# Half a mixer one query block sooner and by seven products, and a shared pair of PSUM banks

## The chip, the cores and the metric

The kernel runs on one core of a Trainium2 chip. The metric is the device time of one execution in microseconds (us), as the median of several executions. TensorE (PE) does the matrix products and their weight loads (PEld), VectorE (DVE) and ScalarE (ACT) empty the PSUM banks, GpSimd (POOL) mostly starts loads, and SyncE (SP) starts transposes by DMA and the stores of the output.

## The reference

Eight batches of 3008 rows go first through a gated attention unit without softmax and then through an MLP-mixer, which works over the rows (tokens) first and over the channels second:

```python
# u, v: (8, 3008, 256), z: (8, 3008, 64), float32
scores = (1.0 / S) * np.matmul(z, z.transpose(0, 2, 1))   # S = 3008
attn = np.maximum(scores, 0.0) ** 2
x = u * np.matmul(attn, v)
# w_tok1 (3008, 256), w_tok2 (256, 3008), w_ch1 (256, 1536), w_ch2 (1536, 256)
h = np.maximum(x.transpose(0, 2, 1) @ w_tok1, 0.0) @ w_tok2
u = x + h.transpose(0, 2, 1)
h2 = np.maximum(u @ w_ch1, 0.0) @ w_ch2
out = (u + h2).astype(np.float32)
```

All products are made in bf16 with sums in float32. Since the scores are symmetric, a block of them that is made for one pair of row blocks serves, transposed, for the other pair too.

## The kernel before

**Blocks.** A batch `b` has six query blocks `q` of 512 rows (the last has 448) and six key groups of four tiles of 128 rows. Below, (b, q) is a query block. `score_run` makes two tiles of a block of scores in one pair of PSUM banks (line 435), `relu` on ACT and `square` on DVE turn them into an `at` tile (lines 473 and 481), and `av_matmul` (line 671) multiplies it with v. From the second batch on, a block of scores above the diagonal is also turned by `flip` (line 540, a DMA transpose on SP) into an `fl` tile for its mirrored pair; the blocks on the diagonal of later query blocks are made as triangles (lines 461, 513, 525). When all six groups of a query block are summed, ACT and DVE add the two halves (lines 798, 804) and gate with u (line 828), and SP turns the result (line 843) into `x_sb`.

**The mixer** of a batch needs all six of its query blocks. Its pieces wait in two lists. `heads` holds `tok1` (line 889, six pieces) and `tok2` (line 908, six pieces; DVE adds their result to xT in line 917, and SP turns that into `u_sb` in line 939). `tails` holds the channel part, six pieces `ch1` for each query block (line 958; their relu goes to ACT in line 1005 or to DVE in line 1007, by which of the two the planner holds to be less loaded), and the second product with w_ch2 in one of two forms:

- the classical form `ch2` (line 1192), four pieces of 12 products of 256 columns for a query block, each two pieces in a PSUM pair `op` of their own, followed by a residual add (line 1206 or 1224) and a store;
- the form `fast` by seven products instead of eight (Winograd's form of Strassen's scheme): 84 products of 128 columns (line 1077) in one PSUM pair `f`, with twelve sums on DVE over h2pre (lines 1030 to 1033) and six adds from `f` (lines 1133 to 1152).

Before the change, `fast` holds for all but the first three query blocks of batch 0 and the very last block. In a batch's last query block (q = 5) only the first 256 rows go by seven products. The rest is classical: one tile of 128 rows in the even batches, and in the odd ones also a tile of the two batches' last 64 rows together. These one or two pieces stand ahead of the products 5, 6, 3 and 7 in the list and take a pair `op`.

**When.** A batch's mixer is made in two halves. The loop at the end of the kernel plans at build time, in the order of PE, with its own estimates of times. `goals` says at which query block which half may start; while a half runs, no attention is picked:

```python
    goals = {(1, 2): (0, 1 + HALF)}
    for b in range(2, B):
        goals[b, 0] = (b - 1, 1 + HALF)
```

So the first half of batch 0 (all of `heads`, and `tails` of its blocks 0 to 2) runs ahead of block (1, 2); from batch 2 on, the second half of the mixer before the last and the first half of the last one run ahead of block (b, 0).

**Room.** There are four PSUM pairs, dealt out by `take_slot`. The twelve `fl` buffers hold both flips and h2pre (three for a query block); `flips_fit` says how many flips may lie in them:

```python
        n = live["fl"] - live["mix"]
        return n < (MIRRORS if b < 2 else AHEAD if in_mixer[0] else ROOM["fl"])
```

with `MIRRORS` 8, `AHEAD` 6 and `ROOM["fl"]` 12. SP's queue is in order; what it starts is planned by `push("sp", ...)`. Loads of u, v and z go by POOL, asked for one at a time, at least 4 us apart (`ask`, `SPACING`).

The functions that the change touches, with the line numbers of the profile:

Of the kernel before, what the change touches and what calls it, by code (L numbers as in the profile page):

```python
# [13 lines left out]
P = 128  # L14
# [43 lines left out]
def kernel(  # L58
# [258 lines left out]
    RES = 6  # L317
    live = {"at": 0, "fl": 0, "xT": 0, "x": 0, "us": 0, "mix": 0, "res": 0}
    ROOM = {"at": 6, "fl": 12, "xT": 9, "x": 6, "us": 3, "res": RES}
    MIRRORS = 8  # L320
    U_TURN = 1
    SUMS_TO_COME = 0.85
    AHEAD = 6
# [207 lines left out]
    def flips_fit(b):  # L531

        n = live["fl"] - live["mix"]
        return n < (MIRRORS if b < 2 else AHEAD if in_mixer[0] else ROOM["fl"])

    def flip(b, q, g, at, uses, done):
        fl = sb.tile([P, GK, QW], BF16, tag="fl", name="fl", bufs=ROOM["fl"])
# [280 lines left out]
    def gate(blk, dh, acc, t):  # L818
        b, q, W = blk.b, blk.q, blk.W
        uT = uTs[b, q]  # L820
        if dh == 0:
            xTs[b, q] = sb.tile([P, DT, QW], BF16, tag="xT", name="xT", bufs=ROOM["xT"])
            live["xT"] += 1
            if W < QW:
                nc.gpsimd.memset(xTs[b, q][:, :, W:], 0.0)
        xT = xTs[b, q]
        full, rest = W // P, W % P
        nc.vector.tensor_mul(  # L828
            xT[:, dh, :full * P].rearrange("p (t s) -> p t s", s=P),
            acc[:, :full * P].rearrange("p (t s) -> p t s", s=P),  # L830
            uT[:, :full, dh, :])
        if rest:
            nc.vector.tensor_mul(
                xT[:, dh, full * P:W], acc[:, full * P:W], uT[:, full, dh, :rest])
        if dh == DT - 1:
            gated[0] += 1
            push("sp", t, 1.25, 7.5 if q < NQ - 1 else 12.0, lambda t: turn_x(b, q, t), first=1,
                 room=lambda: has_room(("x",)) and (b == 0 or mode[0] == "full"))

    def turn_x(b, q, t):  # L840
# [30 lines left out]
    def add_mixer(b):  # L871
# [143 lines left out]

        def fast(q):

            return (b > 0 or q >= NQ // 2) and (b, q) != (B - 1, NQ - 1)

        def columns(q):  # L1020
            return P if q == NQ - 1 else 2 * P
# [31 lines left out]
        PLACE = {1: (0, 0), 6: (0, 0), 7: (0, 0), 4: (0, 1), 2: (1, 0), 5: (1, 1), 3: (1, 1)}  # L1053
        LEFT = {1: (0, 0), 2: (1, 0), 4: (1, 1), 7: (0, 0), 5: (0, 1), 6: (1, 1), 3: (1, 0)}

        def apart(inst, q, writes, bank):

            other = "reads" if writes else "writes"
            own = "writes" if writes else "reads"
            key = f"f{b}_{q}_"  # L1060
            tc.declare_no_dep(inst.ins, group=f"{key}{other}{1 - bank}", reason="other bank")
            tc.add_to_no_dep_group(f"{key}{own}{bank}", inst.ins)

        def matmuls(q, m, c2):

            n = columns(q)
            r, h = PLACE[m]
            to = regions(q)[:, r, h]
            h2, k = st["h2", q, c2 // 2], c2 % 2
            i, half = LEFT[m]  # L1070
            lhs = h2[:, 2 * k + i, half * n:half * n + n]
            if m in (1, 2, 3):
                rhs = w_ch2_sb[:, 2 * c2 + (m > 1), P * (m == 3):P * (m == 3) + P]
            else:
                rhs = w_sums[:, {5: 0, 6: 1, 7: 2, 4: 3}[m], c2, :]
            for j in range(n // P):
                apart(nc.tensor.matmul(  # L1077
                    to[:, j, :], lhs[:, j * P:(j + 1) * P], rhs,
                    start=m in (1, 2) and c2 == 0 and j == 0, stop=c2 == CHT // 2 - 1,
                    skip_group_check=True), q, True, r)  # L1080
# [20 lines left out]
        def piece_over(q):  # L1101
            left[q] -= 1
            if not left[q]:
                n = CHT // 4
                live["fl"] -= n
                live["mix"] -= n
                fl_free.extend([pe[0] + 0.2] * n)

        def done_with_u(q):
            u_left[q] -= 1  # L1110
# [2 lines left out]
        def adds(q, m, end):  # L1113

            us, J, n = st["u", q], columns(q) // P, full_tiles[q]
            f = regions(q)
            a, fifth_at, fourth_at = f[:, 0, 0, :J], f[:, 1, 1, :J], f[:, 0, 1, :J]

            def res(r):
                if st["res", q][r] is None:  # L1120
                    live["res"] += 1
                    st["res", q][r] = sb.tile([P, 2, D], F32, tag="res", name="res", bufs=RES)
                return st["res", q][r].rearrange("p t (h d) -> p t h d", d=P)[:, :J]

            def put(r):
                recent[0] = st["res", q][r][:, 0, :1]
                nc.sync.dma_start(
                    out=rows_of(out[b], q)[:, r * J:(r + 1) * J, :],
                    in_=st["res", q][r][:, :J, :])
                live["res"] -= 1  # L1130

            def first():
                return nc.vector.tensor_add(res(0)[:, :, 0], a, us[:, 0, :J])

            def fifth():
                return nc.vector.tensor_add(res(1)[:, :, 1], fifth_at, us[:, 1, J:2 * J])

            def fourth():
                return nc.vector.tensor_add(res(1)[:, :, 0], fourth_at, us[:, 0, J:2 * J])

            def sixth():
                return nc.vector.tensor_add(res(0)[:, :, 1], a, us[:, 1, :J])

            def third():
                o = res(0).rearrange("p t h d -> p h t d")
                inst = nc.vector.tensor_add(o, f[:, 1, :, :J], o)  # L1146
                put(0)
                return inst

            def seventh():  # L1150
                o = res(1).rearrange("p t h d -> p h t d")
                inst = nc.vector.tensor_add(o, a.unsqueeze(1).to_broadcast([P, 2, J, P]), o)
                put(1)
                return inst

            busy = 0.16 + 0.00105 * J * P * (1 + (m in (3, 7)))
            fn = {1: first, 5: fifth, 4: fourth, 6: sixth, 3: third, 7: seventh}[m]
            after_ = {7: (5, 4), 3: (1, 6)}.get(m, ())

            def room():  # L1160
                if m in (1, 5, 4) and st["res", q][m != 1] is None and not has_room(("res",)):
                    return False
                return all(read[q, k].t is not None for k in after_)

            def run(t):
                apart(fn(), q, False, PLACE[m][0])
                st["reads", q].append(t)
                if m in (3, 7):
                    free["sp"] = max(free["sp"], t) + 0.4
                if len(st["reads", q]) == 6:  # L1170
                    st["freed", q].t = max(st["reads", q])
                    done_with_u(q)

            push("dve", max(end + 0.21, known(st["turned", q])), busy, busy + 0.13, run,
                 first=1, done=read[q, m], room=room)

        def ch2(q, half, i, end):
            apart = alone(q, half)
            if i == 0 or apart:
                st["o_slot"], _ = take_slot()  # L1180
# [80 lines left out]
        def ch2_pieces(q, key):  # L1261
            out = []
            for half in halves(q)[1 if fast(q) else 0:]:
                for i in range(pieces_of(q, half)):
                    two = not alone(q, half)
                    needs = [Sooner(h2_done[q, c2], 0.218 * c2) for c2 in range(CHT // 2)]
                    out.append(Piece(1.312, needs + w_done[2:],
                                     lambda end, half=half, i=i: ch2(q, half, i, end),
                                     opens=two and i == 0, closes=two and i == 1, key=key))
            return out  # L1270

        def products(q, key):
# [8 lines left out]
            def piece(m):  # L1281
                k = {5: 1, 6: 2, 7: 3, 3: 4}[m]
                needs = w_done[2:] + [sums_done]
                needs += [Sooner(s_done[q, c4, k], 2 * one * c4) for c4 in range(CHT // 4)]
                before = {5: (), 6: (1, 4), 3: (5,), 7: (6,)}
                needs += [read[q, k] for k in before[m]]
                return Piece(CHT // 2 * one, needs, lambda end: product(q, m, end),
                             opens=m != 7, closes=True, key=key)

# [2 lines left out]
        for q in range(NQ):  # L1292
# [5 lines left out]
                    s_done[q, c4, k] = Done()  # L1298
            for m in range(1, 8):
                read[q, m] = Done()  # L1300
        groups = [range(NQ)] if b == B - 1 else [range(HALF), range(HALF, NQ)]
        for group in groups:
            key = (b, 2 + group[-1])
# [2 lines left out]
            d = {q: ch2_pieces(q, key) if not fast(q) or q == NQ - 1 else [] for q in group}  # L1306
            for q in group:
                left[q] = (CHT // 4 + 4) * fast(q) + len(d[q])
                u_left[q] = fast(q) + sum(not x.opens for x in d[q])
            q = group[0]  # L1310
            out_pieces = list(c[q])
            if fast(q):
# [7 lines left out]
            for q in group:  # L1320
                if q == group[-1]:
# [2 lines left out]
                        closing.extend(d[q][:2] if b < B - 1 else [])  # L1324
                        break
                    early, m = p[q]
                    out_pieces += [early[2]] + d[q] + [m[5], m[6], m[3], m[7]]
                    closing.extend([early[2], m[6], m[3], m[7]] if d[q] else [
                        early[2], m[5], m[5], m[6]])
                    break  # L1330
# [127 lines left out]
    for b in range(B):  # L1458
# [15 lines left out]
                    at_group(base + NG + 2 * (j // 3) + 14, lambda b=b, j=j: turn_next_z(b, j // 3))  # L1474
        else:
            if b == 1:
                ask_z(2, base + 2 * NG - 1)
            if b + 1 < B:
                last, m = base + NQ * NG - 1, (b + 1) * NQ
                ask_u(m, last)  # L1480
# [102 lines left out]
    late_z(5, 9.0)  # L1583
    first_u(18.5)

    goals = {(1, 2): (0, 1 + HALF)}
    for b in range(2, B):
        goals[b, 0] = (b - 1, 1 + HALF)
    done_units = 2
# [144 lines left out]
```

## Time and profile before

| | us |
|---|---|
| median of 3 runs | 1126.76 |
| lowest and highest of them | 1124.74, 1142.09 |
| the profiled execution | 1127.6 |
| its span, first to last instruction | 1125.8 |
| PE busy (share of the span) | 1108.6 (98%) |
| DVE busy | 754.8 (67%) |
| ACT busy | 664.1 (59%) |
| POOL busy | 152.8 (14%) |

The page of the profile is of the profiled execution, whose time is 1.8 us more than its span. The granted clock of TensorE is 0.999 of full speed. Busy time of PE is from the start of a product to its modelled end, and successive products overlap, so their spacing is read from the distance of their starts or from the chain of work that ended last. A "wait" below is idle time of an engine ahead of an instruction, with what released it.

### The profile page before, as it was taken

The numbers are of one execution on the slowest core, as the hardware profiler recorded it, in microseconds if no ns is written. First come the engines' busy times: TensorE is split into PE (matmuls) and PEld (weight loads), VectorE is DVE, ScalarE is ACT, GpSimd is POOL, SyncE is SP. The second block draws the span as 40 slices with busy tenths as digits, with TensorE's granted clock in tenths as the row PEclk, the third lists the DMA queues.
The fourth block names the chain that finished last, engine by engine and source line by source line (L and its number), as shares of the span: only waits on it lengthen the run. The fifth ranks groups of instructions, "written<-read, shape, count | busy, mean of one in ns | idle before, by whom it ended". The sixth has DMA issues, their size and how long they took to land.

```text
span 1125.8 us, 26158 instructions
## 1 busy us (share of the span) xinstructions
PE 1108.6 (98%) x10604; PEld 688.0 (61%) x10677; DVE 754.8 (67%) x1547; ACT 664.1 (59%) x823; POOL 152.8 (14%) x387
## 2 busy tenths in 40 slices
PE   8999999999999999999999999999999999999998
PEld 3455664666557665676655765567655576556776
DVE  6888655676756767568665686666766667655676
ACT  7999355545855457554675456654566536743464
POOL 4501100222002120021100211002110021000000
PEclk9999999999999999999999999999999999999999
DMA  9999846996969977797896977859689696673212
GB/s 162 182 184 190 152 105 123 161 180 128 183 126 162 164 146 165 134 164 168 143 171 122 188 150 153 180 95 210 137 158 158 113 226 119 136 140 89 71 60 83
DMA packets 470953, 165.48 MB, mean 147 GB/s; under 512 B 433776, under 2 KB 449456, under 8 KB 470832
## 3 DMA queue, kind: packets, MB, share of 16 engines
q1 hardware_dynamic: 442976, 131.11, 57.5%
q0 software_dynamic: 27344, 32.32, 20.0%
q8 instruction: 83, 1.36, 0.5%
q10 hardware_dynamic: 512, 0.38, 0.1%
q14 instruction: 38, 0.31, 0.1%
HBM read 65.40 MB, written 24.64 MB: 80 GB/s over the span
## 4 chain that ended last, share of the span: by engine, by line
PE 93%; DMA 3%; DVE 2%; issue 1%; ACT 1%; SPq 0%; ACTq 0%; DVEq 0%
PE acc L671 39%; PE hp L958 21%; PE f L1077 17%; PE sc L435 6%; PE a_ps L889 4%; PE op L1192 3%; PE h_ps L908 3%; DMA fl<-at 2%; DVE xT L917 1%; PE first_acc L587 1%; DMA zT<-zr 1%; DVE cp L804 0%; DMA zf<-in_z_dram 0%; SPq L540 0%; ACT cp L798 0%
## 5 line engine op out<-in xcount | busy, mean ns | idle before, releaser
L1005 ACT ACTIVATE h2pre<-hp 128x1024 bf16<-128x1024 f32 (+1 forms) x279 | 275.3, 1005 | 240.1 <-PE hp L958 226.1
L671 PEld LDWEIGHTS <-v_sb 64*128 64x128 bf16 x4418 | 249.7, 94 | 207.1 <-issue 0.7
L473 ACT ACTIVATE at<-sc 128x1024 bf16<-128x1024 f32 (+1 forms) x290 | 286.8, 1026 | 89.1 <-PE sc L435 77.4
L671 PE MATMUL acc<-at,v_sb 64*128 64x512 bf16 (+1 forms) x2738 | 339.1, 374 | 0.0
L481 DVE TENSOR_TENSOR at<-at 128x1024 bf16<-128x1024 bf16 (+1 forms) x290 | 198.0, 687 | 129.7 <-ACT at L473 125.6
L958 PE MATMUL hp<-xT,w_ch_sb 128*128 128x512 bf16 (+1 forms) x1090 | 276.8, 374 | 3.2
L1077 PEld LDWEIGHTS <-h2pre 128*128 128x128 bf16 x3402 | 209.7, 98 | 51.0 <-issue 2.2
L671 PE MATMUL acc<-fl,v_sb 64*128 64x512 bf16 (+1 forms) x1680 | 194.0, 367 | 0.1
L1077 PE MATMUL f<-w_sums,h2pre 128*128 128x128 bf16 x1944 | 172.0, 219 | 0.1
L958 PEld LDWEIGHTS <-w_ch_sb 128*128 128x128 bf16 x1152 | 104.7, 98 | 84.9 <-issue 1.0
L435 PE MATMUL sc<-zT 64*128 64x512 bf16 (+1 forms) x732 | 133.1, 359 | 4.4 <-ACT at L461 2.6
L1077 PE MATMUL f<-w_ch_sb,h2pre 128*128 128x128 bf16 x1458 | 119.8, 219 | 0.0
L461 ACT ACTIVATE at<-sc 128x512 bf16<-128x512 f32 (+3 forms) x152 | 55.7, 446 | 59.0 <-PE sc L435 45.0
L804 DVE TENSOR_TENSOR cp<-acc,cp 128x512 f32<-128x512 f32 (+1 forms) x94 | 63.5, 675 | 33.1 <-ACT cp L798 32.8
L798 ACT COPY cp<-acc 128x512 f32<-128x512 f32 (+1 forms) x90 | 52.6, 584 | 44.3 <-PE acc L671 44.2
L513 DVE TENSOR_TENSOR at<-at 128x512 bf16<-128x512 bf16 (+3 forms) x152 | 41.2, 321 | 48.2 <-ACT at L461 48.2
L435 PEld LDWEIGHTS <-zT 64*128 64x128 bf16 x732 | 44.0, 94 | 47.0 <-issue 8.6
L917 DVE TENSOR_TENSOR xT<-xT,h_ps 128x1024 bf16<-128x1024 bf16 (+1 forms) x48 | 56.0, 1173 | 15.4 <-PE h_ps L908 15.1
L1030 DVE TENSOR_TENSOR h2pre<-h2pre 128x512 bf16<-128x512 bf16 (+1 forms) x132 | 52.6, 398 | 19.4 <-PE f L1077 18.8
L828 DVE TENSOR_TENSOR xT<-cp,uT 128x512 bf16<-128x512 f32 (+1 forms) x94 | 62.5, 665 | 1.3
L123 POOL CAST mark<-at 128x1 f32<-128x1 bf16 x13 | 3.5, 265 | 418.5 <-DVE at L481 418.5
L1146 DVE TENSOR_TENSOR res<-f,res 128x512 f32<-128x512 f32 (+1 forms) x44 | 28.6, 649 | 45.9 <-PE f L1077 45.5
(76 smaller groups left out, 699.9 us busy)
## 6 DMA issues: line engine op xcount, KB each, us to landing
out_dram<-res SPq DMA_DIRECT2D x80, 256.0 KB, 2.4
v_sb<-in_v_dram POOLq DMA_DIRECT2D x40, 256.0 KB, 5.9
ur<-in_u_dram POOLq DMA_DIRECT2D x40, 256.0 KB, 4.5
out_dram<-res SPq DMA_DIRECT2D x24, 128.0 KB, 1.8
w_tok_sb<-in_moe_w_tok_dram POOLq DMA_DIRECT2D x10, 256.0 KB, 9.6
zs<-in_z_dram POOLq DMA_DIRECT2D x35, 64.0 KB, 3.0
at<-at SPq DMA_TRANSPOSE x114, 2.4
fl<-at SPq DMA_TRANSPOSE x105, 4.9
```

The source lines that it names most:

```text
L435: nc.tensor.matmul(sc[:, r, c0:c1], zT[h, k:k + P], zT[h, m + c0:m + c1], start=True, stop=True)
L461: nc.scalar.activation(a3[:, i, c0:c1], sc[:, r, c0:c1], ACT.Relu, scale=inv_S)
L473: nc.scalar.activation(view, sv, ACT.Relu, scale=inv_S)
L481: nc.vector.tensor_mul(view, view, view)
L671: nc.tensor.matmul(o, vs[blk.b, g][rows, i, dh * P:(dh + 1) * P], rhs, start=(dh, h) not in blk.begun, stop=stop, skip_group_check=True)
L798: nc.scalar.copy(cp[:, :W], acc[:, 1, :W])
L804: nc.vector.tensor_add(cp[:, :W], acc[:, 0, :W], cp[:, :W])
L828: nc.vector.tensor_mul(xT[:, dh, :full * P].rearrange("p (t s) -> p t s", s=P), acc[:, :full * P].rearrange("p (t s) -> p t s", s=P), uT[: ...
L917: nc.vector.tensor_add(to, to, h[:, :, :n * P].rearrange("p h (s t) -> p h t s", t=n))
L958: nc.tensor.matmul(hp[:, r, :W], w_ch1_sb[:, dc, cc * P:(cc + 1) * P], xT[:, dc, :W], start=(dc == 0), stop=(dc == DT - 1))
L1005: nc.scalar.activation(h2[:, :, :W], hp[:, :, :W], ACT.Relu)
L1077: apart(nc.tensor.matmul(to[:, j, :], lhs[:, j * P:(j + 1) * P], rhs, start=m in (1, 2) and c2 == 0 and j == 0, stop=c2 == CHT // 2 - 1, s ...
```

## The change

Batch 0's first half is allowed one query block sooner (`goals`), and its blocks 0 to 2 go by seven products too (`fast`). Up to that point `flips_fit` allows 6 flips and not 8, and from then on batches 0 and 1 get what the later ones get. The z of batch 2 is asked for one query block sooner, and the planner's estimate for the landing of batch 0's last x is 7.5 us and not 12. In every `fast` last query block the classical rest (new function `rest`) is summed into the unused half of the columns in the pair `f`: the first piece into the second bank, the second piece into the first bank. It takes no pair `op`; the second piece stands behind product 5, and product 3 (or 6) waits for the read of the first (or second) piece. `apart` is renamed `banked`.

```diff
-    MIRRORS = 8
+    MIRRORS = 6
...
-        return n < (MIRRORS if b < 2 else AHEAD if in_mixer[0] else ROOM["fl"])
+        before_mixer = b < 2 and goal[0] < (0, 0)
+        return n < (MIRRORS if before_mixer else AHEAD if in_mixer[0] else ROOM["fl"])
...
-            push("sp", t, 1.25, 7.5 if q < NQ - 1 else 12.0, lambda t: turn_x(b, q, t), first=1,
+            push("sp", t, 1.25, 7.5 if q < NQ - 1 or b == 0 else 12.0, lambda t: turn_x(b, q, t), first=1,
...
-            return (b > 0 or q >= NQ // 2) and (b, q) != (B - 1, NQ - 1)
+            return (b, q) != (B - 1, NQ - 1)
...
+        def read_over(q, t):
+            st["reads", q].append(t)
+            if len(st["reads", q]) == 6 + (pieces_of(q, 1) if q == NQ - 1 else 0):
+                st["freed", q].t = max(st["reads", q])
...
+        def rest(q, i, end):
+            r = 1 - i
+            op = st["f", q].rearrange("p r (h j d) -> p r h j d", h=2, d=P)[:, r, :, 1, :]
+            n = full_tiles[q]
+            k = n - 1 + i
+            for cc in range(CHT):
+                h2 = pair["hs"][:, cc, :] if i else (
+                    st["h2", q, cc // 4][:, cc % 4, k * P:(k + 1) * P])
+                banked(nc.tensor.matmul(
+                    op, h2, w_ch2_sb[:, cc, :].rearrange("p (h d) -> p h d", d=P),
+                    start=False, stop=cc == CHT - 1, skip_group_check=True), q, True, r)
+            piece_over(q)
+            def residual(t):
...
+                for rows, u_rows, to in ends:
+                    banked(nc.vector.tensor_add(
+                        res[rows, i, :].rearrange("p (h d) -> p h d", d=P),
+                        op[rows], u_rows), q, False, r)
+                    nc.sync.dma_start(out=to, in_=res[rows, i, :])
+                free["sp"] = max(free["sp"], t) + 0.4 * len(ends)
+                read_over(q, t)
+                done_with_u(q)
+            busy = 0.43 * (1 + i)
+            push("dve", max(end + 0.21, known(st["turned", q])), busy, busy + 0.13, residual,
+                 done=read[q, "rest", i])
+
         def ch2(q, half, i, end):
+            if fast(q):
+                return rest(q, i, end)
...
+                    if fast(q) and i:
+                        needs += [read[q, 1], read[q, 4]]
...
+                if q == NQ - 1:
+                    needs += [read[q, "rest", i] for i in range(pieces_of(q, 1))
+                              if m == (3, 6)[i]]
...
-                    out_pieces += [early[2]] + d[q] + [m[5], m[6], m[3], m[7]]
+                    out_pieces += [early[2]] + d[q][:1] + [m[5]] + d[q][1:] + [m[6], m[3], m[7]]
...
-                ask_z(2, base + 2 * NG - 1)
+                ask_z(2, base + NG - 1)
...
-    goals = {(1, 2): (0, 1 + HALF)}
+    goals = {(1, 1): (0, 1 + HALF)}
```

More of the change, by code (lines that the diff above doesn't have):

```diff
@@ L1054, in add_mixer, with banked @@
         LEFT = {1: (0, 0), 2: (1, 0), 4: (1, 1), 7: (0, 0), 5: (0, 1), 6: (1, 1), 3: (1, 0)}
-        def apart(inst, q, writes, bank):
+        def banked(inst, q, writes, bank):
             other = "reads" if writes else "writes"
@@ L1076, in matmuls @@
             for j in range(n // P):
-                apart(nc.tensor.matmul(
+                banked(nc.tensor.matmul(
                     to[:, j, :], lhs[:, j * P:(j + 1) * P], rhs,
@@ L1165, in run @@
             def run(t):
-                apart(fn(), q, False, PLACE[m][0])
-                st["reads", q].append(t)
+                banked(fn(), q, False, PLACE[m][0])
                 if m in (3, 7):
                     free["sp"] = max(free["sp"], t) + 0.4
-                if len(st["reads", q]) == 6:
-                    st["freed", q].t = max(st["reads", q])
+                read_over(q, t)
+                if m == 7:
                     done_with_u(q)
@@ L1175, in adds @@
                  first=1, done=read[q, m], room=room)
+        def rest(q, i, end):
[6 more added lines that the diff above has]
+                    st["h2", q, cc // 4][:, cc % 4, k * P:(k + 1) * P])
+                banked(nc.tensor.matmul(
+                    op, h2, w_ch2_sb[:, cc, :].rearrange("p (h d) -> p h d", d=P),
+                    start=False, stop=cc == CHT - 1, skip_group_check=True), q, True, r)
+            piece_over(q)
+            def residual(t):
+                us = st["u", q]
+                if i == 0 and b % 2 == 0:
+                    pair["ut"] = sb.tile([TAIL, DT, P], BF16, tag="ut", name="ut", bufs=1)
+                    nc.gpsimd.tensor_copy(pair["ut"][:], us[:TAIL, :, n, :])
+                res = sb.tile([P, 2, D], F32, tag="res", name="res", bufs=RES)
+                if not i:
+                    ends = [(slice(0, P), us[:, :, k, :], rows_of(out[b], q)[:, k, :])]
+                else:
+                    lower, upper = slice(0, TAIL), slice(TAIL, P)
+                    ends = [(lower, pair["ut"][:], last_rows(out[b - 1])),
+                            (upper, us[upper, :, n, :], last_rows(out[b]))]
+                for rows, u_rows, to in ends:
[4 more added lines that the diff above has]
+                free["sp"] = max(free["sp"], t) + 0.4 * len(ends)
+                read_over(q, t)
+                done_with_u(q)
+            busy = 0.43 * (1 + i)
+            push("dve", max(end + 0.21, known(st["turned", q])), busy, busy + 0.13, residual,
+                 done=read[q, "rest", i])
         def ch2(q, half, i, end):
+            if fast(q):
+                return rest(q, i, end)
             apart = alone(q, half)
@@ L1264, in ch2_pieces @@
                 for i in range(pieces_of(q, half)):
-                    two = not alone(q, half)
+                    two = fast(q) or not alone(q, half)
                     needs = [Sooner(h2_done[q, c2], 0.218 * c2) for c2 in range(CHT // 2)]
+                    if fast(q) and i:
+                        needs += [read[q, 1], read[q, 4]]
                     out.append(Piece(1.312, needs + w_done[2:],
                                      lambda end, half=half, i=i: ch2(q, half, i, end),
-                                     opens=two and i == 0, closes=two and i == 1, key=key))
+                                     opens=two and (i == 0 or fast(q)),
+                                     closes=two and (i == 1 or fast(q)), key=key))
             return out
@@ L1300, in add_mixer @@
                 read[q, m] = Done()
+            for i in range(2):
+                read[q, "rest", i] = Done()
         groups = [range(NQ)] if b == B - 1 else [range(HALF), range(HALF, NQ)]
@@ L1308, in add_mixer @@
                 left[q] = (CHT // 4 + 4) * fast(q) + len(d[q])
-                u_left[q] = fast(q) + sum(not x.opens for x in d[q])
+                u_left[q] = 1 + len(d[q]) if fast(q) else sum(not x.opens for x in d[q])
             q = group[0]
```

## The prediction

> **What bounds the kernel.** I read first the busy times on the page, then PE's waits, then the chain of work that ended last, and last the stretches around the places that the change touches. From the page and from PE's waits over the whole execution:
>
> ```profile
> PE 1108.6 (98%) x10604; PEld 688.0 (61%) x10677; DVE 754.8 (67%) x1547; ACT 664.1 (59%) x823; POOL 152.8 (14%) x387
> ...
> PE sc L435 <- ACT at L461: 2.6, 2, 1.9
> PE op L1192 <- DVE xT L917: 2.2, 5, 0.4
> ...
> PE h_ps L908 <- ACT a_sb L896: 0.7, 1, 0.7
> PE h_ps L908 <- DVE xT L917: 0.5, 1, 0.5
> ```
>
> PE sets the time: it is idle for 1125.8 - 1108.6 = 17.2 us, and some 7 of these lie ahead of 13 us and behind the last product at 1121.7, which the change leaves alone. So a change can win PE work that it removes and the few waits above; it can lose any amount by new waits. The waits read: us in total, times, longest. Two are of interest: five waits of 0.43 us ahead of the classical rest (L1192) and one of 1.9 us ahead of scores.
>
> The chain of waits gives the price of each form of product, since there its pieces stand end to end:
>
> ```profile
> 141.10 5.24 PE op L1192 x48
> ...
> 272.21 2.02 PE f L1077 x36
> ```
>
> A classical product of 256 columns takes 5.24 / 48 = 0.1092 us, one of the seven of 128 columns 2.02 / 36 = 0.0561 us, weight loads included.
>
> The stretches, from the query of busy time by windows (length, PE, PEld, DVE, ACT, POOL, clock, DMA share, GB/s):
>
> ```profile
> 112.40:156.70 44.30, 43.40 (x296) 28.80 (x298) 23.06 (x25) 13.82 (x15) 3.95 (x10) 1.00 0.68 128
> 156.70:203.70 47.00, 45.05 (x431) 22.82 (x430) 26.34 (x48) 28.52 (x40) 3.53 (x9) 1.00 0.69 127
> 203.70:274.20 70.50, 69.46 (x692) 48.92 (x702) 51.58 (x120) 38.70 (x40) 16.29 (x44) 1.00 0.83 158
> ```
>
> The first is batch 0's first half, the second the attention behind it, the third a mixing stretch that is all by seven products. There DVE is busy 51.58 / 70.50 = 73% of the time and PE still 98.5%.
>
> **A: seven products in three blocks.** 3 x 48 products go, 3 x 84 come: 144 x 0.1092 = 15.72 us against 252 x 0.0561 = 14.14 us. On PE, which sets the end: -1.6 us. The rate is that of rows of the same shape, so I give it 0.2 either way.
>
> The skill speaks against this: "TensorE: Matmul & The Clock Gate", section "Back-to-back issue gap", holds that in streams of a weight load and a product each 128-column product costs about 81 ns. By that the 252 would take 20.4 us, 4.7 more than the classical form; the trace has 56 ns with a weight load for every product, and the trace decides.
>
> **A's price on DVE.** 36 sums at 0.424 us (groups by form: 47.2 us over 111 in L1031) are 15.3 us; twelve adds at 0.42 and six at 0.69 replace six residual adds at 0.69: +5.0. DVE in the half: 23.06 + 20.3 = 43.4 us if the relus stay where they are. Eight of these are on DVE now:
>
> ```profile
> L1007 DVE TENSOR_SCALAR h2pre<-hp x8: 1224/1225/1225, 123.1 to 149.9; 128x1024 bf16<-128x1024 f32 x8
> ```
>
> All eight of the kernel lie in this half; wherever `fast` holds, the planner gives DVE a handicap of 0.85 us and all its relus have gone to ACT. So 9.8 us leave DVE (33.6 us, 76% of some 44.4) and 8 x 1.02 = 8.2 join ACT (22.0, 50%). These are the shares of the third stretch, where the DVE work hides behind PE. There PE lost 0.5 us (L908 behind L917 at 239.6), while `tok2` and seven products shared DVE; here they share it too, and three blocks' product chains wait for sums. Cost taken: +0.5 us; bounds 0 and +2.5 (three blocks, each with its last four sums, 1.7 us, of which a `ch1` piece covers 0.87). The relus of two more `ch1` pieces are drawn ahead into this half and missing in the next one: no PE work gained or lost.
>
> **B: the rest in the pair f.** Ten pieces of 12 products (one in the four even batches 0 to 6, two in 1, 3 and 5) need no pair `op`. The wait was this:
>
> ```profile
> 511.94 1.47 PE L1192 MATMUL op<-w_ch_sb,h2pre 128*128 128x256 bf16 x12 [0.43 <-DVE xT L917]
> ```
>
> All four pairs were held, one by a `tok2` result that DVE was still adding. Now the piece starts at once: up to 5 x 0.43 = -2.2 us. What is late next is the following `tok2` piece, which wants the same pair, 1.31 us later; by then the add has ended (the wait was 0.43). DVE, however, is busy nearly without a break from 506 to 516 in that stretch, so part of the stall may come back ahead of product 5. I take -1.4; bounds -2.7 (with the 0.5 of L908 above) and 0.
>
> Its price: the output of a product is now two runs of 128 columns. No row has that; the nearest are one run of 256 (0.1092) and two products of 128 (0.1122), so 120 x 0.003 = +0.4 us at most, and 0 taken, by the row of 256. The skill's page "PSUM — Partial Sum Buffer", section "Specifications (TRN2)", says that a non-contiguous pattern slows products significantly, with no figure; if it doubled them that would be 120 x 0.109 = 13.1 us. No run here shows it.
>
> **New waits of B.** In the odd batches product 6 waits for the read of the second piece: 0.21 us to DVE, an add of 128 rows and two of 64 at 0.42 = 1.3 us, behind one xT add of 1.22 at worst: 0.2 to 2.7 us, covered by one `ch1` piece and one `tok2` piece between (0.87 each). Queued behind it on PE are products 3 and 7, the next batch's `tok2` and `ch1`, and for these ACT and DVE wait. In the even batches product 3 waits for the first piece, with products 5 and 6 and two more pieces between: nothing. Three times 0 to 0.9: +0.4 taken, bounds 0 and +2.7. The stores (one, or three in odd batches) are as many as before on SP.
>
> **C: one block sooner.** The 296 PE instructions of the half move ahead of block (1, 1), from 112.4 to about 100.9; attention of (1, 1) and its successors follows. With it move six stores, three turns of u, and, by `ask_z`, eight z loads on POOL and five z turns on SP. They pass on SP three flips of (1, 1), which the limit of 6 now holds back (nine were started from 86 to 115.7, the last three in 8.25 us from 107.47) and on POOL the load of u for (1, 3), which goes from 104.2 to about 149; its user, the gate of (1, 3), lies near 180, and a turn takes 3.7 us to land. Is everything there at 100.9? The last x of batch 0 was issued at 92.05 and landed 5.8 us later; the weight sums ended at 97.9 (L1543 to L1546). So the sooner start costs no PE wait, but the margin is 3 us; without it PE would stand idle, as attention is not picked. The exposed evacuation of `a_ps` (0.7 us) stays, as nothing can go beside it.
>
> What C may win is the stall of the second stretch:
>
> ```profile
> 179.21 1.43 ACT L461 ACTIVATE at<-sc 128x512 bf16<-128x512 f32 x4 [7.51 <-DMA fl<-at]
> ...
> 180.24 0.37 PE L435 MATMUL sc<-zT 64*128 64x512 bf16 x2 [1.89 <-ACT at L461]
> ```
>
> ACT waited 7.5 us for an `at` buffer that a flip still held; the flip waited for room, 8 in batch 1. The limit after the half is now that of later batches, where the same place costs 0.7 us at 317, 0.2 near 597 and nothing elsewhere. I take -1.5 of 1.9, bounds -1.9 and +1 (the three flips come behind the half, 8 us of SP, under about 10 us of attention in the `at` tiles that are ready; what shows if they are late is scores again, by up to 1).
>
> **Sum** against the profiled execution: 1127.6 - 1.6 + 0.5 - 1.4 + 0.4 - 1.5 = 1124.0 us. The median before is 0.8 under that execution, so 1123.2; I say **1123.5**. All favourable ends give 1127.6 - 1.8 - 2.7 - 1.9 = 1121.2, and runs of one kernel lie up to 2.9 us under the profiled one.
>
> **Rivals.**
> 1. *A wash.* B's stall comes back on a busy DVE and C's moves to another block: only A is left and 0.5 + 0.4 + 0.5 against it, 1127.4. For it: DVE's unbroken work around 511. Against: later batches run C's limit with hardly a stall.
> 2. *Slower: DVE bounds the first half.* If the relus stay on DVE, it has 43.4 us of work in 44.4, and each block's last sums and adds (4 x 0.42 + 0.42 + 0.69 = 2.8 us) are exposed behind its products: 8.4 us, and the waiting is on PE. 1127.6 - 1.6 - 2.9 + 8.4 = 1131.5. It decides once these waits exceed 4.5 us. Against: the third stretch.
> 3. *It does not start sooner*: x or the sums come late in the plan, PE idles up to 4.5 us (the 12 less the 7.5 us). 1124.0 + 4.5 = 1128.5. Against: the landing at 97.9.
> 4. *More*: all stalls named go and none comes: 1121.2.
>
> **Chances.** Forecast 0.58, wash 0.17, DVE 0.10, late start 0.05, more 0.10. The range must hold the forecast's cases (1120 to 1126), the wash and most of rival 2: 1118.5 to 1131.5. A measurement of this kernel tells about 2% (22.5 us) from no change. Faster by more would need more than PE's whole idle time of 17.2 us: 0.01. Slower by more needs a mechanism that no row shows: 0.05. Within: 0.94.
>
> **What would show it.** Right (lines by their names of before): L1077 with 252 more products, L1192 with 48 in the last block and 120 in `rest`; no L1007; `a_ps` of batch 0 near 101; no wait of L1192 on L917; PE's wait on L461 under 1 us; PE busy down by 1.6. Wrong: waits of L1077 on L1030 to L1033 or on adds from `f`, of L889 on a DMA near 101, or spaced products of the rest (over 0.115 us each).

## The result, and the profile after

| | median, us (lowest to highest, runs) | ratio to the kernel before, 95% interval |
|---|---|---|
| before | 1127.0 (1124.74 to 1142.09, 6) | |
| after | 1120.1 (1119.95 to 1137.69, 6) | 0.9939 [0.9923, 0.9956] |
| after, on another chip (`whole_again`) | 1121.03 (1120.14 to 1123.05, 6) | 0.9942 [0.9928, 0.9955] |

The changed kernel is 0.6% faster, by 6.5 to 7 us; 1123.5 was forecast. The profile of after shown here is that of `whole_again`, because the profiled execution of the first run had a granted clock of 0.992 (and those of the experiments `sooner_old_room` and `no_a` had 0.995 and 0.949, so that of these only the names and numbers of the waits are read).

Its span is 1118.4 us, against 1125.8 before. Its line of busy times, and all of its groups of PE's waits:

```profile
PE 1110.1 (99%) x10785; PEld 682.8 (61%) x10785; DVE 760.7 (68%) x1587; ACT 672.0 (60%) x831; POOL 153.5 (14%) x387
...
PE acc L672 <- DVE cp L805: 1.5, 3, 0.5
PE wp L198 <- DVE zero L1440: 1.2, 1, 1.2
PE sc L435 <- DMA zT<-zr: 0.7, 1, 0.7
PE h_ps L909 <- ACT a_sb L897: 0.7, 1, 0.7
```

PE's idle time is 1118.4 - 1110.1 = 8.3 us. That must not be compared with the 17.2 of before: that trace has 10604 products beside 10677 weight loads, so it lacks 73, and this one has all. The 73 are 62 of `hp`, 9 of `h_ps` and 2 of `first_acc`, all of 512 columns, by the groups of instructions; these three groups read 4.1 us busier in the trace of `rest_only`, which has the same products and lacks none. So PE's idle time before was some 13 us, and the prediction's 17.2 is too much by what the trace lacks. The waits can be compared. They came to 9.1 us before (2.6 on L461, 2.2 on L917 ahead of the rest, and smaller ones) and are 4.1 now. The two waits on L461, the five of the rest and the 0.5 us of `h_ps` on xT are all gone. New are three waits of 0.5 us of `acc` on the copy `cp`.

The stretches that answer to the three of before (length, PE, PEld, DVE, ACT, POOL, clock, DMA share, GB/s): the first half of batch 0, the attention behind it, and the mixing stretch.

```profile
99.80:143.00 43.20, 42.51 (x398) 28.64 (x397) 31.51 (x64) 23.28 (x25) 4.41 (x10) 1.00 0.66 130
143.00:196.00 53.00, 53.00 (x511) 25.32 (x510) 34.39 (x60) 37.12 (x49) 3.27 (x8) 1.00 0.91 160
196.00:267.00 71.00, 71.00 (x711) 48.57 (x706) 52.26 (x121) 38.07 (x40) 16.41 (x44) 1.00 0.83 155
```

In the first half DVE is busy 31.51 / 43.20 = 73% of the time, the share that the mixing stretch had before, and the only gap of PE is the 0.69 us of `a_sb`. In the other two PE has no gap at all; before, the second had 1.95 us and the third 1.04 (of which 0.52 is the wait of `h_ps` on xT; the trace lacks ten products there). The groups of instructions say where the relus went; the eight of DVE have no row any more, and all 287 are ACT's:

```profile
L1006 ACT ACTIVATE h2pre<-hp 128x1024 bf16<-128x1024 f32 (+1 forms) x287 | 282.8, 1005 | 226.6 <-PE hp L959 215.7
```

The timeline of PE at the start of the first half, and at the rest of a last query block (the place that was at 511.94 before):

```profile
98.52 1.04 PE L672 MATMUL acc<-at,v_sb 64*128 64x512 bf16 x8
99.50 2.25 PE L890 MATMUL a_ps<-x_sb,w_tok_sb 128*128 128x256 bf16 x19
...
505.26 0.22 PE L1078 MATMUL f<-w_sums,h2pre 128*128 128x128 bf16 x1
505.32 1.47 PE L1191 MATMUL f<-w_ch_sb,h2pre 128*128 128x256 bf16 x12
506.63 1.03 PE L909 MATMUL h_ps<-w_tok_sb,a_sb 128*128 128x512 bf16 x4
```

A wait would stand in square brackets at the end of a line; there is none. `a_ps` starts 12.9 us sooner than before (112.42), behind the last `acc` without a gap. The twelve products of the rest take 506.63 - 505.32 = 1.31 us, 0.109 each.

A wait costs a little more than its idle time, since the product ahead of it counts as busy up to its modelled end. Before, the product ahead of the rest was this:

```profile
511.29 0.22 PE L1077 MATMUL f<-w_sums,h2pre 128*128 128x128 bf16 x1
```

From its start to the start of the rest at 511.94 it was 0.65 us, and now it is 505.32 - 505.26 = 0.06. So the stall cost 0.59 us where 0.43 were counted as idle. By this place, some 0.16 us for each wait that is gone is hidden in PE's busy time, an estimate.

### The profile page after: what moved, and what is told of

Its sections match the earlier page's. It is cut to its first block, busy times and chain, and to the rows that moved or that the text cites. A ratio compares the mean times of both kernels' runs of the same rounds, so it can differ in the third digit from the quotient of the medians.

```text
span 1135.9 us, 26518 instructions
## 1 busy us (share of the span) xinstructions
PE 1114.7 (98%) x10785; PEld 681.8 (60%) x10785; DVE 760.6 (67%) x1587; ACT 672.7 (59%) x831; POOL 153.5 (14%) x387
## 4 chain that ended last, share of the span: by engine, by line
PE 90%; DMA 7%; ACT 1%; POOL 1%; DVE 1%; issue 0%; SPq 0%; POOLq 0%
PE acc L672 36%; PE hp L959 21%; PE f L1078 18%; PE sc L435 5%; PE a_ps L890 4%; PE h_ps L909 4%; DMA w_tok_sb<-in_moe_w_tok_dram 3%; PE f L1191 1%; DMA zT<-zs 1%; DMA zs<-in_z_dram 1%; DMA v_sb<-in_v_dram 1%; DMA ur<-in_u_dram 1%; ACT at L473 1%; PE op L1237 0%; PE wp L198 0%; DMA uT<-ur 0%
## 5 line engine op out<-in xcount | busy, mean ns | idle before, releaser
L1006 ACT ACTIVATE h2pre<-hp 128x1024 bf16<-128x1024 f32 (+1 forms) x287 | 282.8, 1005 | 226.6 <-PE hp L959 215.7
L672 PEld LDWEIGHTS <-v_sb 64*128 64x128 bf16 x4418 | 244.4, 94 | 217.7 <-issue 6.1
L473 ACT ACTIVATE at<-sc 128x1024 bf16<-128x1024 f32 (+1 forms) x290 | 287.7, 1026 | 105.7 <-PE sc L435 99.0
L672 PE MATMUL acc<-at,v_sb 64*128 64x512 bf16 (+1 forms) x2738 | 343.0, 377 | 0.0
L959 PE MATMUL hp<-xT,w_ch_sb 128*128 128x512 bf16 (+1 forms) x1152 | 281.7, 375 | 0.0
L1078 PEld LDWEIGHTS <-h2pre 128*128 128x128 bf16 x3654 | 225.0, 98 | 55.3 <-issue 2.6
L1078 PE MATMUL f<-w_sums,h2pre 128*128 128x128 bf16 x2088 | 184.5, 219 | 0.0
L1078 PE MATMUL f<-w_ch_sb,h2pre 128*128 128x128 bf16 x1566 | 128.5, 219 | 0.0
L461 ACT ACTIVATE at<-sc 128x512 bf16<-128x512 f32 (+3 forms) x152 | 55.0, 446 | 41.8 <-PE sc L435 39.5
L1031 DVE TENSOR_TENSOR h2pre<-h2pre 128x512 bf16<-128x512 bf16 (+1 forms) x141 | 56.4, 400 | 18.9 <-PE f L1078 17.6
L1033 DVE TENSOR_TENSOR h2pre<-h2pre 128x512 bf16<-128x512 bf16 (+1 forms) x141 | 56.6, 401 | 9.1
```

What stands on the lines that cost most here:

```text
L473: nc.scalar.activation(view, sv, ACT.Relu, scale=inv_S)
L672: nc.tensor.matmul(o, vs[blk.b, g][rows, i, dh * P:(dh + 1) * P], rhs, start=(dh, h) not in blk.begun, stop=stop, skip_group_check=True)
L959: nc.tensor.matmul(hp[:, r, :W], w_ch1_sb[:, dc, cc * P:(cc + 1) * P], xT[:, dc, :W], start=(dc == 0), stop=(dc == DT - 1))
L1006: nc.scalar.activation(h2[:, :, :W], hp[:, :, :W], ACT.Relu)
L1031: (3, lambda: nc.vector.tensor_sub(a11, a11, a21)),
L1033: (2, lambda: nc.vector.tensor_sub(a22, a22, a11)),
```

## The experiments

Four theories were put against each other. **Parts add**: each part wins the PE work or the waits that it removes. **Room alone**: the new limit of flips does what seems to come from the sooner start and the seven products. **Overlap**: two parts remove the same stall. **DVE bounds the first half**: the prediction's rival 2.

The yardstick first: the kernel before, measured against itself.

> The kernel before, unaltered, for a second profile: that of before has gaps in its record of PE products and a granted clock of 0.9994. Both theories: waits of PE within 0.5 us of the first profile in each line but those on DMA at the start; what differs is not the change. If the 1.9 us of the scores near 178 differs by more, then part of what I put down to the limits on flips is the spread of one kernel.

Measured: 1127.17 us, ratio 0.9985 [0.9963, 1.0007]. Its waits are those of before within 0.2 us. So the waits named in these two profiles repeat, while ratios that differ by under 0.002 are not told apart. The ratio is not that of the two medians: here the medians, 1127.17 and 1127.8, would give 0.9994. `room_only`, `sooner_old_room` and `not_sooner` have the same runs of before as this yardstick, and are best read against its 0.9985. All medians, with the ratio to runs of before on the same chip:

| kernel | parts of the change in it | median, us | ratio, 95% interval |
|---|---|---|---|
| `room_only` | limit of flips | 1126.16 | 0.9976 [0.9951, 1.0001] |
| `sooner_old_room` | sooner | 1128.15 | 0.9996 [0.9976, 1.0017] |
| `sooner_with_room` | limit, sooner | 1125.45 | 0.9976 [0.9967, 0.9986] |
| `seven_with_room` | limit, seven products | 1124.19 | 0.9967 [0.9954, 0.9979] |
| `rest_only` | rest in `f` | 1123.52 | 0.9964 [0.9950, 0.9977] |
| `no_b` | all but the rest in `f` | 1123.10 | 0.9963 [0.9951, 0.9975] |
| `no_a` | all but the seven products | 1123.45 | 0.9955 [0.9938, 0.9971] |
| `not_sooner` | all but sooner | 1122.44 | 0.9950 [0.9928, 0.9972] |
| `whole_again` | all | 1121.03 | 0.9942 [0.9928, 0.9955] |
| `relu_dve` | all, 9 relus of the half on DVE | 1125.93 | 0.9977 [0.9961, 0.9992] |
| `margin03` | all, another choice of the next piece | 1124.80 | 0.9976 [0.9965, 0.9987] |

### The whole change again

> The changed kernel unaltered, for a profile at full clock to set against the one of before. Theory 1 (the three parts add up, each by the wait or the work that it takes away): 1120 us, the waits of the classical rest on the xT add (5 x 0.43 us) and of the scores on the triangle's relu (1.9 us) gone, the scores' 0.7 us near 317 and the xT wait of 0.5 us near 240 gone too, and nothing new above 1 us. Theory 2 (only the extra room for flips counts): the waits of the classical rest are still there in another line. Either way PE's busy time falls by about 1.6 us, or by more if busy time held hidden waits.

Measured: ratio 0.9942, as in the first measurement; its profile is the one above.

### Only the rest in the pair f

Edit: `rest`, `read_over` and the order of the pieces; nothing else of the diff.

> Part B alone: the classical rest in the pair f, all else as before. Theory 1: the five waits of 0.43 us go, 2.2 us, and some of the 0.5 us near 240; 1127.0 - 2.2 = about 1124.8. Theory 2 (B's stall comes back ahead of product 5 or 6, since DVE is busy without a break there): 1127.0, with new waits of the seven products' line on DVE of some 2 us in total.

Measured: 0.9964, -4.1 us. PE's waits:

```profile
PE sc L435 <- DMA zT<-zr: 1.3, 1, 1.3
PE sc L435 <- ACT at L461: 1.3, 1, 1.3
PE wp L198 <- DVE zero L1439: 1.2, 1, 1.2
PE acc L671 <- DVE cp L804: 1.0, 2, 0.5
PE h_ps L908 <- ACT a_sb L896: 0.7, 1, 0.7
PE acc L671 <- DMA fl<-at: 0.2, 1, 0.2
```

The five waits of 0.43 us are gone and did not come back at product 5 or 6: no line has `f`. Gone too are the 0.5 of `h_ps` and the second of the two waits on L461 (0.7 us at 319.9), far from the rest; why is not settled. The first, at 179 and so ahead of every rest, reads 1.3 here, 1.9 before and 1.7 in `before_again`; that is no gain of the rest. Two waits of `acc` on `cp` are new. The named waits fall from 9.1 to 5.7 us, 3.4 of the 4.5 us between the two spans. As there are five waits fewer (`issue`, which only traces with products missing have, left out), most of the last 1.1 us is the 0.16 hidden in each, 0.8 us.

### Only the limit of flips

```diff
-    MIRRORS = 8
+    MIRRORS = 6
-        return n < (MIRRORS if b < 2 else ...)
+        before_mixer = b < 2 and goal[0] < (0, 0)
+        return n < (MIRRORS if before_mixer else ...)
```

> Of part C only the new limits on flips (6 before the mixer, then 6 while blocks of h2pre are taken and 12 else); the half starts ahead of (1, 2) as before. Theory 1 (the stall near 178 is a flip that waits for the limit of 8): it shrinks to under 1 us, 1127.8 - 1.0 to 1.9 = about 1126.2. Theory 2 (the stall goes because the half moved): it stays, 1127.8. Theory 3 (6 before the mixer is the harm): it grows, 1129.

Measured: 0.9976, just not told apart from 1, and only 0.0009 (1.0 us) under the yardstick. The stall of 1.9 us near 180 is gone, but one of 1.4 stands at 318.4, where 0.7 stood before, and one of 0.8 on L473 at 303.7:

```profile
PE op L1193 <- DVE xT L918: 2.2, 5, 0.4
PE sc L435 <- ACT at L461: 1.4, 1, 1.4
PE wp L198 <- DVE zero L1388: 1.2, 1, 1.2
PE sc L435 <- ACT at L473: 0.8, 1, 0.8
```

So the limit alone moves the stall: the waits of scores on L461 and L473 are 2.2 us, against 2.8 before. That speaks against the room theory, that the limit does most of the work; by time alone, with so wide an interval, it is not refuted.

### The sooner start with the old limit, and with the new one

```diff
-    goals = {(1, 2): (0, 1 + HALF)}
+    goals = {(1, 1): (0, 1 + HALF)}
...
-                ask_z(2, base + 2 * NG - 1)
+                ask_z(2, base + NG - 1)
```

and the 7.5 us for the last x; in the second kernel the limit as well.

> Of part C all but the new limits: the half ahead of (1, 1), z sooner, 7.5 us; 8 flips throughout batches 0 and 1; classical blocks, the rest in its own pair. Theory 1 (the limit makes the stall): a stall of some 1 to 2 us on the scores stays somewhere between 140 and 200, 1126 to 1127.8. Theory 2 (the moved half takes it away by itself): the same time as part C whole, 1125.4.

> Part C alone: the half ahead of block (1, 1), the new limits on flips, z of batch 2 sooner, the planner's 7.5 us; classical blocks 0 to 2 and the rest in its own pair, as before. Theory 1: only the stall of 1.9 us goes, 1125.1, with the five waits of 0.43 us as before. Rival (sooner start costs: x or weight sums late): an idle PE of some 3 us near 101, 1128 or more.

Measured: 0.9996 with the old limit, 0.9976 with the new one. Starting sooner shows no gain by itself; with the old limit two waits on L461 stay. With the new one a single wait of 0.7 on L461 is left (at 316.4), 1.5 us less of such waits than in `room_only`, but the ratio is the same. In time, what the sooner start adds to the limit is within the error.

### Seven products with the new limit

```diff
-            return (b > 0 or q >= NQ // 2) and (b, q) != (B - 1, NQ - 1)
+            return (b, q) != (B - 1, NQ - 1)
```

and the limit, since with the old one h2pre would find no `fl` buffer.

> Part A with the new limits on flips (6 before the mixer, later the general limits), without which the plan for three more blocks by seven products runs out of buffers; the half still starts ahead of block (1, 2). Theory 1: 252 x 0.0561 in place of 144 x 0.1092 us gives -1.6, and the new limit takes away most of the 1.9 us stall near 178: 1127.0 - 3.5 = about 1123.5. Rival (DVE bounds the half): waits of the seven products on their sums or adds of over 4 us in this half, and 1127 or more.

Measured: 0.9967, 1.0 us under `room_only` by the ratios, where 1.6 us of PE work went. A sixth wait of the rest appears (2.6 us over six), that of `h_ps` on xT is gone, and L461 falls to 0.5. The gain is of the right size, and it isn't told apart from zero by time alone.

### All but the sooner start

Edit: the limit, the seven products and the rest; `goals`, `ask_z` and the 7.5 us stay as before.

> All of the change but the sooner start (the half ahead of (1, 2), the estimate of 12 us and the asking for z as before); the limits on flips are the new ones. Theory 1: the parts add up, so the whole without the sooner start is 1121.0 + 0.8 to 1.3 (what is left of the stalls of (1, 3) and (1, 4) when the half lies ahead of (1, 2)) = about 1122. Theory 2 (the sooner start is what makes the seven products of the first half come free): 1124.

Measured: 0.9950 against 0.9942 for the whole: not told apart. Its profile has a wait of 0.4 on L473 at 183.5 and one of 0.7 on `cp` at 185.4, so the stretch that once held the 1.9 us still holds 1.1 without the sooner start. `rest_only` and `seven_with_room` together would be -4.1 - 3.7 = -7.8 us; measured -5.6, or -4.0 against the yardstick. The parts overlap, or the intervals hide that they add.

### All but the rest in f, all but the seven products

> The whole change without the rest in the pair f: the classical rest of the last block takes a pair of its own, as before. If the parts add: the rest alone won 4.3 us, so 1125.3, with five waits of op on xT of some 0.43 us back (2.2 us in all) and none of acc on the DVE copy (1.5 us). If the gain of the rest overlaps with that of the new limit (the landmarks of the batches showed -2.0 at the last batch for the limit alone, -4.6 for the rest alone, -7.4 for all): between 1123 and 1125. Not under 1123 by either.

> The whole change without the seven products in batch 0's first three blocks, which keep the classical form; first half sooner, rest in the pair f, new limit of flips. Kernel before 1127.8, whole change 1121.0 so far. If the parts add, each by the PE work or the wait that it removes: this loses only the 1.65 us of PE work of the seven products, about 1122.7, with the same waits as the whole change. If the seven products cost something on DVE in the first half that the other parts pay for: no slower than the whole, 1121.0 or under. If the parts overlap and room alone did most of the sooner-and-seven gain: 1122 to 1123, not to be told from the first.

Measured: `no_b` 0.9963, 2.3 us over the whole change by the ratios, where the rest alone had won 4.1. Its time lies in the overlap's 1123 to 1125 and not at strict addition's 1125.3; but the 4.1 and the 2.3 have errors of 1.5 us and more, so time alone doesn't settle it. `no_a` 0.9955, 1.5 us over the whole, the size of the 1.6 us of PE work, though the interval of that difference includes zero. PE's waits in `no_b`:

```profile
PE op L1193 <- DVE xT L918: 2.6, 6, 0.4
PE sc L435 <- DMA zT<-zr: 1.9, 1, 1.9
PE wp L198 <- DVE zero L1388: 1.2, 1, 1.2
PE sc L435 <- DMA zT<-zs: 1.0, 1, 1.0
PE sc L435 <- ACT at L473: 0.7, 2, 0.4
...
PE sc L435 <- DVE cp L805: 0.3, 1, 0.3
```

Here the overlap can be read: no wait on L461, though the rest still has its own pair. What the rest wins in company is 2.6 + 0.7 + 0.3 of waits less the 1.5 of `acc` on `cp`, 2.1 us, beside 2.3 measured. The waits on DMA (`zr`, `zs`) lie ahead of 85 us, before any rest, and are left out. Over all kernels the pattern is plain: wherever the rest is in `f`, the waits of the rest are gone and two or three waits of `acc` on `cp` are there (`rest_only`, `no_a`, `not_sooner`, `relu_dve`, `margin03`, the whole); wherever it isn't, five or six waits of 0.43 are there and none of `acc` on `cp`.

### DVE given half of the relus back

The whole change, but in batch 0's blocks 0 to 2 every second relu goes to DVE:

```diff
-            on_act = load("act") + 0.92 < load("dve") + 1.15 + SUMS_TO_COME * fast(q)
+            on_act = (load("act") + 0.92 < load("dve") + 1.15 + SUMS_TO_COME * fast(q)) if (b > 0 or q >= NQ // 2) else c2 % 2 == 0
```

> The whole change, but in batch 0's blocks 0 to 2 every second relu (9 of 18) goes to DVE instead of ACT. DVE has 31.5 us of work in the 43.2 us of the first half in the whole change; 9 relus of 1.225 us bring it to about 42.5, which is the state that rival 2 of the prediction assumed. Rival 2 (DVE then bounds the half, sums and adds are exposed): 5 to 9 us over the whole change, 1126 to 1130, with waits of f on the sums or on adds from f in the half. Theory that PE hides DVE work there up to nearly the whole half: within 1.5 us of the whole change, 1121 to 1122.5.

Measured: 0.9977, 3.9 us over the whole change. PE's waits, and its timeline in the half:

```profile
PE acc L672 <- DVE cp L805: 1.5, 3, 0.5
PE f L1078 <- DVE h2pre L1008: 1.5, 2, 1.0
PE f L1078 <- DVE h2pre L1033: 1.4, 2, 0.8
...
123.54 0.40 PE L1078 MATMUL f<-w_sums,h2pre 128*128 128x128 bf16 x4 [0.75 <-DVE h2pre L1033]
130.84 0.40 PE L1078 MATMUL f<-w_ch_sb,h2pre 128*128 128x128 bf16 x4 [0.44 <-DVE h2pre L1008]
134.89 0.40 PE L1078 MATMUL f<-w_sums,h2pre 128*128 128x128 bf16 x4 [0.69 <-DVE h2pre L1033]
141.91 0.40 PE L1078 MATMUL f<-w_ch_sb,h2pre 128*128 128x128 bf16 x4 [1.02 <-DVE h2pre L1008]
```

Each block's products now wait for DVE, for a relu (L1008) or for the sums behind it (L1033): with 0.2 on L1032 and 0.4 on an ACT relu, 3.5 us in the half, which is nearly the whole loss. DVE is busy for 37.69 us of 99.80 to 143.00, where it was 31.51. The mechanism of rival 2 exists; it stands at sums and relus only, not at adds from `f`, and it costs less than half of the 8.4 us that were named for it, with DVE somewhat less loaded than the rival's 43.4 of 44.4 us. It did not happen because the planner's handicap put the relus on ACT.

### Another choice ahead of acc

An attempt on the three new waits, and on a faster kernel: the planner counts a PSUM pair as free in time only with 0.3 us to spare.

```diff
-        by_then = [s for d, s in ring if (guess.get(s, FAR) if d.t is None else d.t) <= need]
+        by_then = [s for d, s in ring if (guess.get(s, FAR) if d.t is None else d.t) <= need - 0.3]
```

> The whole change, but the planner counts a PSUM slot as free in time for the next need only where it is so 0.3 us sooner, so that fewer score units are taken just ahead of acc. If the three new waits of 0.5 us of acc on the DVE copy come from that choice and nothing takes their place: 1119.5. If the order of the whole execution, which shifts with it in every batch, brings other waits of the same size: 1120.5 to 1123. Slower than 1123 only if score units taken later leave PE without attention to do.

Measured: 0.9976, slower than the whole change by 3.8 us. PE's waits:

```profile
PE acc L672 <- DVE cp L805: 2.5, 3, 1.5
PE sc L435 <- DMA zT<-zr: 1.8, 1, 1.8
PE sc L435 <- ACT at L473: 1.2, 2, 0.9
```

The three waits stay, one of them at 1.5 us, and two on L473 join them. In the timeline of `whole_again` all three look alike. At the first, ACT's copy (304.48, 0.58 us) and then DVE's add (305.29, 0.68 us) read `acc`; PE has run out of other work 0.51 us before the add is done, and the next `acc` starts behind it, at 306.02. Why the rest in `f` brings this about is not settled, and no kernel run here beats the whole change.

## Why the prediction was right or wrong

The kernel is faster by under 2% and in the range, but the forecast of 1123.5 is 2.5 to 3.4 us too high. The time is that of rival 4, 1121.2, "all stalls named go and none comes", partly by luck: the stalls that B and C name went, but 1.5 us of new ones came, and other terms made up for these. Step by step:

- **A, PE work: right.** -1.6 was said. The seven products of the new blocks run at 2.02 us for 36 in the chain of work (the line below), 0.0561 each; `no_a` puts the part at 1.5 us, with a wide interval. The trace, with 56 ns, thus goes against the skill's 81 ns ("TensorE: Matmul & The Clock Gate", "Back-to-back issue gap") in these blocks too.

```profile
141.90 2.02 PE f L1078 x36
```

- **A's price on DVE: mis-sized, 0 for the +0.5 taken.** That all relus would leave DVE was right (no row of DVE, 23.28 us on ACT where 22.0 was said, DVE 31.51 for 33.6). PE has no wait on a sum in the half.
- **B: mis-sized, the step "part of the stall may come back".** -1.4 was taken of 2.2; all of the 2.2 went, and the 0.5 of `h_ps` as well, the favourable bound of 2.7. Product 5, which takes the place of the late `tok2` piece, never waited.
- **Price of the two runs of the output: right at 0.** Twelve products in 1.31 us are 0.109 each, as with one run of 256 columns. The skill's "any non-contiguous AP slows matmuls significantly" ("PSUM — Partial Sum Buffer", "Specifications (TRN2)"; an AP is an access pattern) is not seen at runs of 128 float32 columns.
- **New waits of products 3 and 6: 0 for the +0.4.** No wait of L1078 on a read is in the profile.
- **C: mis-sized, -2.6 for -1.5.** The 1.9 us near 180 went entirely, as at the favourable bound, and so did the 0.7 us at 319.9 (317 in the prediction), which the working gave as normal for the new limit and didn't count. The named cause was incomplete: the limit alone moved the stall (1.4 at 318.4), the sooner start alone left it, and the rest alone removed one of the two. Among the kernels here, no wait on L461 is left only where the limit stands with at least two of the other three parts. That a margin of 3 us in the landing of x is enough was right: no wait of `a_ps`. Rival 3 did not happen.
- **Missing from the sum: +1.5**, three waits of `acc` on `cp` that come with the rest in `f`. The working named `tok2` and product 5 as what is late next; it was the attention behind the mixing stretch (at 306, 580 and 854).
- **Rival 2** did not happen, but `relu_dve` shows that its mechanism is real, at 3.5 us and not 8.4.
- **PE busy down by 1.6** can't be read against the page of before, which lacks 73 products. Traces that lack none show it roughly: 1112.5 in `sooner_with_room` and 1111.4 in `seven_with_room`, 1111.4 in `rest_only` and 1110.1 in the whole change. Rival 1, the wash, did not happen: neither stall came back at its own place.

The balance of the two profiles: the prediction's sum, from the profiled execution before and with the sizes as measured, is 1127.6 - 1.6 - 2.7 - 2.6 + 1.5 = 1122.2 us, and the profiled execution of the changed kernel took 1120.2. Of the 2.0 us between, 0.8 is the wait `zT<-zr` at the start of the kernel, which reads from nothing (`sooner_with_room`) to 1.9 us (`no_b`) in the kernels here, though no part touches it; it is no gain of the change. 0.2 is a wait on L473 that is gone. The last 1.0 us is the 0.16 hidden in each of the six waits that are gone on balance (again without `issue`), an estimate from the one place shown above.

## What to carry to other kernels

Where one engine is busy 98% of the time, a change is worth the work and the waits that it removes, and the waits here sat in shared buffers: a limit on them alone moved the stall, and it went only together with other parts of the change. Count all waits of a kind when one cause is removed, also those far from the edit, and look for the next one in the stage that follows, not only at the neighbouring instruction. A change that adds work to a second engine depends on which engine takes the movable work beside it: half of the relus on the wrong engine cost 3.9 of the 7 us.

## What the runs showed of the hardware that was not expected

A product that writes two separate runs of 128 float32 columns into a PSUM bank costs no more here than one of 256 in a row: 272 ns from start to modelled end, and 1.31 us (0.109 each) for the twelve of each of the ten pieces, where the chain of work before had 0.1092 for one of 256. Read with the instructions of one line (durations: least, median, largest):

```profile
L1191 PE MATMUL f<-w_ch_sb,h2pre x84: 272/273/273, 231.5 to 1051.0; 128*128 128x256 bf16 x84
L1191 PE MATMUL f<-w_ch_sb,hs x36: 272/273/273, 370.6 to 919.7; 128*128 128x256 bf16 x36
```
